# Attention beside a bilinear GLU on one core: moving the last split weights' store and the stores of the heads' outputs

## The chip, the core and the metric

The kernel runs on one core of a Trainium2 chip. The metric is device time in microseconds (us) of one execution. The kernel before took 2605.79 us, the median of 3 runs (2604.93 to 2606.27). A core has TensorE (PE, matmuls; PEld is its weight load), VectorE (DVE), ScalarE (ACT), GpSimd (POOL) and SyncE (SP). Each engine works through its own instructions in the order in which the program lists them, and waits on semaphores for the others. A DMA is issued by an instruction of SyncE or GpSimd: what stands behind an issue that waits, waits too.

## What is computed

```python
xn = layernorm(x)                        # x: 2048 x 576
q, k, v = split(xn @ wqkv)               # 32 heads of 18
s = concat_heads(softmax(q k^T / sqrt(18)) v) @ wo
h = (xn @ w_gate) * (xn @ w_up)          # 4608 columns
out = x + s * silu(h @ w_down)
```

All is float32. To keep its precision, matmul operands are split into a high part (float32r) and a low part (the rest), and a product is made of three partial products: high by high, high by low and low by high.

## The kernel before, in words

**Stages.** A first stage norms `x`, makes q, k and v and writes them to DRAM (`sqk`, `sv`). The long middle stage interleaves attention and the GLU in one stream of matmuls. The end multiplies the heads' outputs with `wo`, makes the gate's silu and writes the result.

**The GLU** goes over 72 units: 4 chunks of 512 rows of `x` (a pass each) times 18 blocks of 256 columns of F. A unit has two pairs of up and gate products (27 matmuls each, L658), and the down product of the unit before (L700), added to `acc` by DVE (L728). TensorE's upper and lower 64 rows work at the same time on two such streams (`stream(0)` for up, `stream(1)` for gate). The low part of `h` is made by GpSimd (L674); `turn_round` (L690) loads `hs` with its halves exchanged as `hx`.

In pass one (units 0 to 17) the weights are split as they are used: ScalarE makes the high part, GpSimd the low part (L191 for gate and up, L222 for down), and the split weights are stored in DRAM (`swg` at L196, `swd` at L226). The later passes load them (L182, L215). Odd passes take the blocks backwards, so that the unit after a pass turn (18, 36, 54) has the weights of the unit before and keeps its tile (L209 to L212). `d_get(u + 1)` is called in `down_end` when both halves of unit u's down product are listed, and `turn_round(u + 1, 1)` right after it (L735 to L738). At a pass turn the blocks of the next chunk of `x` are loaded, 18 DMAs (L358, L361).

**Attention.** Per head there are 64 "a" matmuls (L582), whose row maxima DVE takes (L584); `max_rows` sends them through GpSimd's queue (L604) into the stacked operands `pair` and `ring`; 64 "b" matmuls (L614), whose exponentials ScalarE takes (L616); and the product with v (L625), listed in visits of 7 blocks of 8 matmuls. `pair` and `ring` are loaded for each head by SyncE (L239). `finish(h)` transposes the head's sum on DVE, divides it by its last column, transposes it back into `oc` (L637 to L642), and stores it to `sot` with four DMAs of 18 rows by 512, one for each quarter of the rows (L645, SyncE).

**The order** is made when the program is written out, by `order()`. It keeps clocks for the two streams and for DVE, ScalarE and GpSimd, and one number, `queue[0]`, for when the DMA queue is through with what was issued. `moved(start, size)` adds a transfer to it at 0.24 MB per us and returns the time of landing, 2 us later. An operation is listed once its data are there by these clocks (`there`, `arrives`, `loaded`). In `visit`, when a head is finished, `queue[0]` is raised to the time at which DVE is through with the finish (L1034). Neither the stores of split weights nor the heads' stores are counted in `queue[0]`.

**The end.** When the last "b" is listed, `begin` puts six loads of the heads' outputs (`fetch_o`, L794) on a list `loads`; when the last visit is listed, `prefetch` adds four `fetch`es (L822, L824). `order()` lists one of them at a time, when `queue[0]` is at most 0.3 us ahead. What is left follows after the order, behind the loads of blocks 3 and 4 of the outputs (L794, L797). ScalarE makes the high part of each block (`high`, L802), DVE the low part (`low`, L807 and L809), `w_split` splits `wo` (L814, L815), and L1210 is the output projection: its first group of 6 products runs over four row tiles and two halves before the second begins.

Of the kernel before, what the change touches and what calls it, by code (L numbers as in the profile page):

```python
# [20 lines left out]
FT = mybir.dt.float32  # L21
# [19 lines left out]
def kernel(  # L41
# [10 lines left out]
    nc = tc.nc  # L52
    _, S, D = x.shape
    F = w_gate.shape[1]
    H = 32
    DH = D // H
# [3 lines left out]
    NF2 = F // 256  # L60
# [14 lines left out]
    swd = dram.tile([NF2, 128, 2, 2, 2, HALF], FT, name="swd")  # L75
    sv = dram.tile([S, H, DH + 1], FT, name="sv")
    sot = dram.tile([D, S], FT, name="sot")
# [49 lines left out]
    def d_tile():  # L127
        return wpool.tile([128, 2, 2, 2, HALF], FR, name="wd", bufs=1)
# [26 lines left out]
    def columns_of(u):  # L155
        c, q = units[u]
        return NF2 - 1 - q if c % 2 else q

    graw, gw, draw, dw = {}, {}, {}, {}
# [41 lines left out]
    def d_load(n):  # L201
        if n < NF2:
            draw[n] = d_raw(n)

    def d_get(n):
        if n >= len(units) - 1:
            return
        p = columns_of(n)
        if n and n % NF2 == 0:  # L209
            dw[n] = dw[n - 1]  # L210
            ddone.add(n)
            return  # L212
        w = dw[n] = d_tile()
        if n >= NF2:
            nc.sync.dma_start(w.bitcast(FT), swd[p])  # L215
            ddone.add(n)
            return
        raw = draw.pop(n)

        def dpiece(k):  # L220
            nc.scalar.activation(w[:, k, :, 0, :], raw[:, k], AF.Copy)
            nc.gpsimd.tensor_tensor(w[:, k, :, 1, :], raw[:, k], w[:, k, :, 0, :].bitcast(FT), op=OP.subtract)  # L222

        def end():
            ddone.add(n)
            nc.sync.dma_start(swd[p], w.bitcast(FT))  # L226
            d_load(n + 1)

        chores.extend([(dpiece, (k,)) for k in range(2)] + [(end, ())])
# [300 lines left out]
    for t in range(8, NT):  # L530
# [6 lines left out]
        if t > 11:  # L537
            for n in range(2 * (t - 12), 2 * (t - 11)):
                x_first(n // 2, n % 2)
    d_get(0)  # L540
    xg.append(xcp.tile([128, 9, 512], FR, name="xc"))
    n = 8
# [21 lines left out]
    with ExitStack() as mid:  # L564
# [55 lines left out]
        def pv_group(h, ts, k):  # L620

            p = bank("g", 1, k)
            for t in ts:
                for c in range(4):
                    nc.tensor.matmul(p[32 * c:32 * c + 32, :], vt[h // 2][:, t, 6 * (h % 2):6 * (h % 2) + 32], pt[t, c],  # L625
                                     start=t == ts[0], stop=t == ts[-1])
            if ts[0] == 0:
                oc[h] = mp.tile([128, 512], FT, name="oc", bufs=2)
                nc.scalar.activation(oc[h], p, AF.Copy)  # L629
            else:  # L630
                nc.vector.tensor_tensor(oc[h], oc[h], p, op=OP.add)  # L631

        def finish(h):
            o = oc.pop(h)
            d0 = 13 * (h % 2)
            tp = mp.tile([128, 512], FT, name="tp", bufs=1)
            nc.vector.transpose(tp, o)  # L637
            tr = tp.rearrange("p (j d) -> p j d", d=32)
            rc = mp.tile([128, NT, 1], FT, name="rc", tag="m", bufs=1)
            nc.vector.reciprocal(rc, tr[:, :, d0 + DH:d0 + DH + 1])  # L640
            nc.vector.tensor_tensor(tr[:, :, d0:d0 + DH], tr[:, :, d0:d0 + DH], rc.to_broadcast([128, NT, DH]), op=OP.mult)
            nc.vector.transpose(o, tp)  # L642

            for c in range(4):
                nc.sync.dma_start(sot[h * DH:(h + 1) * DH, 512 * c:512 * c + 512], o[32 * c + d0:32 * c + d0 + DH, :])  # L645

        hs, us = {}, {}
        TERMS = [t for b in range(9) for t in ((b, b, 0), (9 + b, b, 0), (b, b, 1))]
# [70 lines left out]
        def down_end(r, u, s, ps):  # L719
            c, q = units[u]  # L720
            cs = slice(r * HALF, (r + 1) * HALF)
            if q == 0 and c >= 2:
                ready(sdone, 4 * c - 8 + s)
            a = sums(4 * c + s)[:, cs]
            if q == 0:
                nc.vector.tensor_copy(a, ps[:, 0:HALF])
            else:
                nc.vector.tensor_tensor(a, a, ps[:, 0:HALF], op=OP.add)  # L728
            if q == NF2 - 1 and c < NCH - 1:
                seen[c, s] = seen.get((c, s), 0) + 1  # L730
                if seen[c, s] == 2:
                    silu_store(4 * c + s)
            if s == 3:
                seen[u] = seen.get(u, 0) + 1
                if seen[u] == 2:  # L735
                    d_get(u + 1)
                    if u + 1 < len(units) - 1:
                        turn_round(u + 1, 1)  # L738
# [50 lines left out]
        loads = []  # L789
# [90 lines left out]
        def next_free(tag):  # L880
            if tag == "g":
                return min(banks["g"])
            return banks[tag][turn[tag] % len(banks[tag])]

        def engine(eng, start, taken):
            free[eng] = max(free[eng], start) + taken
            return free[eng] + TAIL[eng]
# [14 lines left out]
        there, queue = {}, [0.0]  # L902
# [98 lines left out]
        def size(first):  # L1001
            h, t, _ = first
            n = h * NT + t
            whole = H * NT - LAST_BLOCKS
            return min(VISIT - n % VISIT, whole - n) if n < whole else 4 - (n - whole) % 4

        shown = [0.0]

        def visit(now):

            now = max(now, *clk)
            many = 0
            now += 0.095
            if due:
                now = max(now, next_free("g") - EARLY + 0.03)
            for h, t, at in due:
                if at > now + 0.5 * many + 0.3 or many == size(due[0]):
                    break
                now += 0.859
                many += 1  # L1020
            now -= 0.859 * many
            for h in sorted({h for h, _, _ in due[:many]}):
                ts = [t for g, t, _ in due[:many] if g == h]
                now = max(now, next_free("g") - EARLY + 0.03) + 0.859 * len(ts)
                k = banks["g"].index(next_free("g"))
                pv_group(h, ts, k)
                end = engine("DVE", now + 0.25, 0.60) if ts[0] else engine("ACT", max(now + 0.25, shown[0]), 0.495)
                banks["g"][k] = end + EARLY
                if ts[-1] == NT - 1:
                    finish(h)  # L1030
                    engine("DVE", end, 0.60)
                    engine("DVE", 0.0, 0.85)
                    shown[0] = engine("DVE", 0.0, 0.60)
                    queue[0] = max(queue[0], shown[0])  # L1034
            del due[:many]
            clk[0] = clk[1] = issued[0] = now + 0.13
            fresh[:] = True, True
# [40 lines left out]
        def order():  # L1078
# [5 lines left out]
            while any(heads) or na < TOTAL or nb < TOTAL or due:  # L1084
# [9 lines left out]
                if len(due) >= need and due[need - 1][2] <= now:  # L1094
                    wait = now if wait is None else wait
                    if abs(clk[0] - clk[1]) < 0.04 or now > wait + 1.0 or not all(heads):
                        visit(now if any(heads) else max([now] + [d[2] for d in due]))
                        wait = None
                        if nb == TOTAL and not due:
                            prefetch(now)  # L1100
                        continue
# [134 lines left out]
    for t in range(NT):  # L1236
# [5 lines left out]
        for _ in range((2, 0, 0, 0, 2, 2, 1, 0, 2, 2, 1, 0, 0, 0, 0, 0)[t]):  # L1242
            if split:
                k, c = split.pop(0)
# [35 lines left out]
```

## Time and profile before

| | before |
|---|---|
| median of 3 runs | 2605.79 us (2604.93 to 2606.27) |
| the profiled execution | 2606.23 us |
| its span, first to last instruction | 2604.5 us |
| granted TensorE clock, mean | 0.998 |
| busy: TensorE / DVE / ScalarE / GpSimd | 99% / 74% / 56% / 20% |
| read from and written to HBM | 312.21 MB, 107.61 MB |
| DMAs `sot<-oc`, L645 | 128, 36 KB each |
| DMAs `swd<-wd`, L226 | 18, 1152 KB each |

The profile is of one execution; its times count from the first instruction (us). A group of rows names line, engine and operation, then output <- input. "[3.86 <-DMA ring<-sqk]" behind an instruction says how long its engine stood idle before it and who released it. A trailing "q", as in SPq, is an engine's queue of semaphore and DMA-issuing instructions, which are not counted as busy. The granted clock is the share of full speed that TensorE was given.

### The profile page before, as it was taken

Reading aid. Unit: us, or ns where it says so; the run is one execution under the profiler, and the core shown is the slowest. Engines: PE = TensorE matmul, PEld = TensorE weight load, DVE = VectorE, ACT = ScalarE, POOL = GpSimd, SP = SyncE. Lnnn points to the kernel's source line nnn. Section 1 sums busy time; section 2 is a strip of 40 time slices with the busy share of each in tenths; the row PEclk is TensorE's granted clock in tenths of the full one; section 3 lists DMA queues with packets and bytes.
Section 4 is the critical chain, followed back from the end, with each engine's and each line's share of the span. In section 5 each row is a group of like instructions: output and inputs, shape, how many; then the busy total and the mean of one; then the engine's idle time right before and its main releaser. Section 6 shows DMA issues by size and latency. Waiting matters only on the chain.

```text
span 2604.5 us, 59060 instructions
## 1 busy us (share of the span) xinstructions
PE 2579.5 (99%) x24360; PEld 2115.4 (81%) x24360; DVE 1920.7 (74%) x3373; ACT 1462.6 (56%) x2698; POOL 526.3 (20%) x534
## 2 busy tenths in 40 slices
PE   8999999999999999999999999999999999999999
PEld 7899888788878888887888888877888888777879
DVE  6208777777767888877788788777788888777537
ACT  5222666666655555655555565655555665555551
POOL 3114433333311111101111111111010111111116
PEclk9999999999999999999999999999999999999999
DMA  7799989888785556565676556556685666655557
GB/s 234 224 287 269 268 225 225 229 217 222 218 204 164 175 178 178 172 179 165 177 191 178 165 173 182 176 164 174 158 204 154 176 184 175 177 175 167 152 165 251
DMA packets 194814, 504.57 MB, mean 194 GB/s; under 512 B 56360, under 2 KB 114344, under 8 KB 155504
## 3 DMA queue, kind: packets, MB, share of 16 engines
q1 hardware_dynamic: 188160, 492.15, 67.6%
q0 software_dynamic: 6384, 8.63, 1.2%
q8 instruction: 192, 3.15, 0.5%
q14 instruction: 78, 0.64, 0.1%
HBM read 312.21 MB, written 107.61 MB: 161 GB/s over the span
## 4 chain that ended last, share of the span: by engine, by line
PE 96%; DMA 2%; DVE 1%; issue 1%; ACT 1%; POOL 0%; SPq 0%; POOLq 0%; ACTq 0%; DVEq 0%
PE pg L658 34%; PE pg L625 17%; PE pg L700 15%; PE pa L582 11%; PE pb L614 9%; PE pg L392 2%; PE pa L338 2%; PE pb L338 2%; PE pg L1210 1%; PE pa L1210 1%; PE pb L1210 1%; DMA ring<-sqk 0%; DMA hx<-hs 0%; ACT xn L286 0%; DMA xc<-sx 0%
## 5 line engine op out<-in xcount | busy, mean ns | idle before, releaser
L584 DVE TENSOR_REDUCE mx<-pa 128x1 f32<-128x512 f32 x2048 | 1361.7, 684 | 161.5 <-PE pa L582 73.8
L616 ACT ACTIVATE pt<-pb 128x512 f32<-128x512 f32 x2048 | 1155.0, 597 | 567.8 <-PE pb L614 468.7
L658 PE MATMUL pg<-xc,wgu 64*128 64x512 f32 x7776 | 1396.6, 392 | 0.0
L658 PEld LDWEIGHTS pg<-xc,wgu 64*128 64x128 f32 x7776 | 1057.5, 186 | 45.5 <-issue 0.2
L614 PE MATMUL pb<-pair,ring 56*128 56x512 f32 x2006 | 788.9, 399 | 4.0 <-DMA ring<-sqk 3.9
L582 PE MATMUL pa<-pair,ring 54*128 54x512 f32 x2001 | 784.7, 398 | 0.3 <-DVE mx L584 0.3
L700 PE MATMUL pg<-wd,hs 64*128 64x288 f32 x3408 | 536.4, 292 | 1.2 <-DVE acc L728 1.2
L700 PE MATMUL pg<-wd,hx 64*128 64x288 f32 x3408 | 528.1, 292 | 1.3 <-DMA hx<-hs 1.2
L674 POOL TENSOR_TENSOR hs<-us,hs 128x512 fp32r<-128x512 f32 x144 | 186.3, 1294 | 1484.1 <-ACT hs L673 1442.9
L700 PEld LDWEIGHTS pg<-wd,hs 64*128 64x128 f32 x3408 | 473.5, 186 | 5.9 <-DVE acc L728 1.9
L700 PEld LDWEIGHTS pg<-wd,hx 64*128 64x128 f32 x3408 | 467.3, 185 | 5.2 <-DMA hx<-hs 2.0
L625 PE MATMUL pg<-pt,vt 128*32 128x512 f32 x4096 | 456.5, 596 | 0.0
L582 PEld LDWEIGHTS pa<-pair,ring 54*128 54x128 f32 x2001 | 363.4, 184 | 82.9 <-issue 48.6
L614 PEld LDWEIGHTS pb<-pair,ring 56*128 56x128 f32 x2006 | 364.7, 184 | 15.1 <-issue 5.1
L625 PEld LDWEIGHTS pg<-pt,vt 128*32 128x32 f32 x4096 | 125.9, 110 | 285.6 <-issue 282.0
L631 DVE TENSOR_TENSOR oc<-oc,pg 128x512 f32<-128x512 f32 x69 | 47.4, 687 | 325.2 <-PE pg L625 314.3
L728 DVE TENSOR_TENSOR acc<-acc,pg 128x288 f32<-128x288 f32 x544 | 233.8, 443 | 27.0 <-PE pg L700 24.2
L673 ACT ACTIVATE hs<-us 128x512 fp32r<-128x512 f32 x144 | 91.0, 632 | 154.5 <-DVE us L670 148.9
L191 POOL TENSOR_TENSOR wgu<-wraw,wgu 128x384 fp32r<-128x384 f32 x108 | 108.4, 1017 | 96.7 <-ACT wgu L190 66.3
L629 ACT ACTIVATE oc<-pg 128x512 f32<-128x512 f32 x32 | 19.2, 599 | 189.4 <-PE pg L625 183.6
L604 POOL DMA_DIRECT2D pair<-mt x128 | 76.6, 604 | 225.1 <-DVE mt L599 223.8
L670 DVE TENSOR_TENSOR us<-pg,us 128x512 f32<-128x512 f32 x144 | 98.2, 682 | 17.9 <-PE pg L658 14.4
(127 smaller groups left out, 1292.4 us busy)
## 6 DMA issues: line engine op xcount, KB each, us to landing
wgu<-swg SPq DMA_DIRECT2D x102, 1152.0 KB
hx<-hs SPq DMA_DIRECT2D x142, 512.0 KB
wd<-swd SPq DMA_DIRECT2D x50, 1152.0 KB
swg<-wgu SPq DMA_DIRECT2D x36, 1152.0 KB
pair<-sqk SPq DMA_DIRECT2D x192, 144.0 KB
ring<-sqk SPq DMA_DIRECT2D x384, 72.0 KB
swd<-wd SPq DMA_DIRECT2D x18, 1152.0 KB
sqk<-hl SPq DMA_DIRECT2D x32, 512.0 KB
```

The source lines that it names most:

```text
L191: nc.gpsimd.tensor_tensor(w[:, 9 + b:12 + b, :], raw[:, b:b + 3, :], w[:, b:b + 3, :].bitcast(FT), op=OP.subtract)
L338: nc.tensor.matmul(p, wq[b, a], xcs[c][:, e, :], start=n == 0, stop=n == len(PAIRS) - 1)
L582: nc.tensor.matmul(p, q[rows, t * 128:(t + 1) * 128], k[rows, c * 512:(c + 1) * 512], start=True, stop=True)
L584: nc.vector.tensor_reduce(mx[h][:, t, c:c + 1], p, axis=AX.X, op=OP.max)
L614: nc.tensor.matmul(p, k[rows, t * 128:(t + 1) * 128], q[rows, c * 512:(c + 1) * 512], start=True, stop=True)
L616: nc.scalar.activation(pt[t, c], p, AF.Exp, scale=scale)
L625: nc.tensor.matmul(p[32 * c:32 * c + 32, :], vt[h // 2][:, t, 6 * (h % 2):6 * (h % 2) + 32], pt[t, c], start=t == ts[0], stop=t == ts[-1])
L658: nc.tensor.matmul(ps, gw[n][half[r], a, :], xg[i][half[r], e, :], start=k == 0, stop=k == len(TERMS) - 1)
L670: nc.vector.tensor_tensor(h32, ps, h32, op=OP.mult)
L674: nc.gpsimd.tensor_tensor(hj[:, 1, :], h32, hj[:, 0, :].bitcast(FT), op=OP.subtract)
L700: nc.tensor.matmul(ps[:, 0:HALF], (hx if k else hs)[u][half[r], j, a, s * 128:(s + 1) * 128], dw[u][half[r], k, j, e, :], start=n == 0, st ...
L728: nc.vector.tensor_tensor(a, a, ps[:, 0:HALF], op=OP.add)
```

## The change

The store of the split down weights of block 17, the last of pass one, is no longer issued in unit 17's `end` but in `d_get(18)`, the first unit of pass two, which keeps the tile. The four stores of a head are issued by GpSimd for the first 31 heads; for the last head they are put on the list `loads` (0.037 MB each), to be issued by SyncE in their turn. The raise of `queue[0]` at the finish of a head is gone.

```diff
@@ d_get
         if n and n % NF2 == 0:
             dw[n] = dw[n - 1]
             ddone.add(n)
+            if n == NF2:
+                nc.sync.dma_start(swd[p], dw[n].bitcast(FT))
             return
...
         def end():
             ddone.add(n)
-            nc.sync.dma_start(swd[p], w.bitcast(FT))
+            if p < NF2 - 1:
+                nc.sync.dma_start(swd[p], w.bitcast(FT))
             d_load(n + 1)
@@ finish
+            def store(c, eng):
+                eng.dma_start(sot[h * DH:(h + 1) * DH, 512 * c:512 * c + 512], o[32 * c + d0:32 * c + d0 + DH, :])
+
             for c in range(4):
-                nc.sync.dma_start(sot[h * DH:(h + 1) * DH, 512 * c:512 * c + 512], o[32 * c + d0:32 * c + d0 + DH, :])
+                if h < H - 1:
+                    store(c, nc.gpsimd)
+                else:
+                    loads.append((store, (c, nc.sync), 0.037))
@@ visit
                     shown[0] = engine("DVE", 0.0, 0.60)
-                    queue[0] = max(queue[0], shown[0])
```

## The prediction

> **What bounds the kernel now.** I read the head of the page, then TensorE's waits over the whole span, then the two places that these waits name: the instructions of SyncE and TensorE in order of time, the chain, and short windows for the clock.
>
> ```profile
> span 2604.5 us, 59060 instructions
> PE 2579.5 (99%) x24360; PEld 2115.4 (81%) x24360; DVE 1920.7 (74%) x3373; ACT 1462.6 (56%) x2698; POOL 526.3 (20%) x534
> ```
>
> TensorE is busy for 99% of the span. A busy TensorE isn't one at its peak, but the order of its work is written out by a planner that always has another matmul to put beside a waiting one. So a DMA or another engine counts only where TensorE stood still for it. All waits of TensorE (engine, line, who was waited for: us in total, times, longest), those from the second row on:
>
> ```profile
> PE pb L614 <- DMA ring<-sqk: 3.9, 1, 3.9
> PE pa L1210 <- ACT hi L802: 2.1, 2, 1.4
> PE pg L700 <- DMA hx<-hs: 1.2, 1, 1.2
> ```
>
> One score matmul waited once for a load of `ring`, and the output projection waited for `hi` at its start. The third comes at about 281 us, before the first head is finished, where the change touches nothing. Everything rests on the first two.
>
> *The ring wait.* SyncE's DMA issues around it, in order of time (start, us, engine and line):
>
> ```profile
> 755.03 0.35 SPq L226 DMA_DIRECT2D swd<-wd  x1
> 755.43 1.87 SPq L239 DMA_DIRECT2D ring<-sqk  x3
> ```
>
> The three ring loads stand directly behind the store of the last split of down, L226. SyncE's own waits from 750 to 790 us say that this store also held the queue until GpSimd had made the split:
>
> ```profile
> SPq L226 <- POOL wd L222: 3.0, 1, 3.0
> ```
>
> The chain in order of time (start, us, what), an earlier undisturbed visit of PV first:
>
> ```profile
> 733.87 6.15 PE pg L625 x56
> ...
> 756.92 11.12 DMA ring<-sqk
> ...
> 768.79 7.97 PE pg L625 x56
> ```
>
> TensorE's instructions in order of time give the gap, and short windows (us, TensorE busy, granted clock, DMA share, GB/s) what came after it:
>
> ```profile
> 768.39 0.46 PE L614 MATMUL pb<-pair,ring 56*128 56x512 f32 x1 [3.86 <-DMA ring<-sqk]
> ```
>
> ```profile
> 768.00:772.00 4.00, 3.61 (x22) 0.68 0.40 131
> 772.00:776.00 4.00, 4.00 (x36) 0.89 0.02 4
> ```
>
> The wait costs twice: 3.86 us of standing still, and then the clock falls to 0.68, so that the 56 matmuls of the visit take 7.97 us where 6.15 us is normal, 1.82 us more. Together **5.68 us**.
>
> *The start of the output projection.* SyncE and ScalarE at the end of the planned order:
>
> ```profile
> 2522.61 0.45 SPq L794 DMA_DIRECT2D o<-sot  x1
> 2530.09 1.40 SPq L645 DMA_DIRECT2D sot<-oc  x4
> ```
>
> ```profile
> 2527.62 0.63 ACT L802 ACTIVATE hi<-o 128x512 fp32r<-128x512 f32 x1 [3.03 <-DMA o<-sot]
> ...
> 2535.38 0.63 ACT L802 ACTIVATE hi<-o 128x512 fp32r<-128x512 f32 x1 [6.55 <-DMA o<-sot]
> ```
>
> One of the six loads of the heads' outputs goes out at 2522.61; then SyncE stands until 2530.09 before the last head's stores, which wait for the transposes of `finish`. The other five loads queue behind them, and ScalarE waits 6.55 us for the second. What it costs is read off the first group of the projection, 4 row tiles x 2 halves x 6 = 48 matmuls (start of the first, start of the next group, an undisturbed dozen in the chain, and the clock):
>
> ```profile
> 2534.23 0.40 PE L1210 MATMUL pa<-wos,hi 128*128 128x288 f32 x1
> ...
> 2545.22 0.95 PE L1210 MATMUL pa<-wos,o 128*128 128x288 f32 x6
> ```
>
> ```profile
> 2546.96 1.59 PE pg L1210 x12
> ```
>
> ```profile
> 2538.00:2542.00 4.00, 3.86 (x19) 0.63 0.99 315
> ```
>
> A dozen takes 1.59 us, so 48 need 6.36; they took 10.99. **4.63 us** are lost, part waits and part the clock of 0.63.
>
> **A page against the rows.** The Trainium skill, page "TensorE: Matmul & The Clock Gate", section "What's actually happening", lets the clock fall to half after an idle window of about 3.4 us. The ring wait agrees with that; at the projection the longest single wait was 1.4 us and the clock fell all the same. Taken strictly, the rule would leave the end only its waits of some 2.3 us (an estimate) and the sum near 8.0 instead of 10.3; the row with 0.63 decides.
>
> **The change part by part.**
>
> *Last split's store in pass two.* It removes from L226 one DMA and with it the 3.0 us of SyncE's wait. Its size, and the rate of the stretch before the gap (windows; the last two figures are DMA share and GB/s):
>
> ```profile
> swd<-wd SPq DMA_DIRECT2D x18, 1152.0 KB
> ```
>
> ```profile
> 755.00:768.40 13.40, 9.54 (x84) 9.03 (x80) 8.89 (x14) 7.39 (x13) 1.29 (x2) 1.00 0.98 260
> ```
>
> The DMA engines are full (0.98), so what counts is bytes ahead, not the earlier issue: 1152 KB are 1.18 MB, at 260 GB/s 4.5 us. The load landed at 768.04 and would land at 763.5; TensorE wants it at 768.39 - 3.86 = 764.5. The wait goes, with 1 us to spare, and nothing else was late: the following visit had its data. From both sides: nothing, if the later loads crowd in; 5.68 at most. I take 5.68, since the bytes stand ahead in the same queue. If a rest of a microsecond stays, it costs only itself: the 1.2 us wait for `hx` left the clock alone.
>
> ```profile
> 278.00:282.00 4.00, 2.75 (x32) 1.00 0.98 308
> ```
>
> The store comes back in `d_get(18)`, called by `down_end` of unit 17 just ahead of the next `hx` issue:
>
> ```profile
> 790.50 1.11 SPq L690 DMA_DIRECT2D hx<-hs  x2
> ```
>
> ```profile
> 810.57 0.29 PE L700 MATMUL pg<-wd,hs 64*128 64x288 f32 x1
> ```
>
> It puts 4.5 us ahead of that `hx`, whose first reader starts at 810.57, 20 us after the issue. In every other unit of the later passes a load of the same size stands there. It costs nothing; without that cover it would cost 4.5 us.
>
> *Stores of 31 heads through GpSimd.* SyncE loses 124 issues and its longest class of waits that isn't for a buffer:
>
> ```profile
> SPq L645 <- DVE oc L642: 197.0, 29, 13.4
> ```
>
> That is 6.8 us a head by which loads behind can go earlier. Since TensorE waited for a load only twice in the whole planned stage, this gains nothing now. GpSimd takes on 124 DMA issues. Its nearest row (shortest, median and longest ns of one, first and last start in us):
>
> ```profile
> L604 POOL DMA_DIRECT2D pair<-mt x128: 594/597/769, 250.6 to 2445.3; - x128
> ```
>
> 124 x 0.597 = 74 us on an engine that is busy for 526 of 2604; 2.4 us a head. GpSimd now stands before the stores until DVE's transposes are through, and behind them in its queue wait `hs` low parts, in pass one the splits (L191, L222), `silu`'s products, and `pair<-mt`. What stood behind one head's stores (SyncE's row, then GpSimd's):
>
> ```profile
> 779.78 1.36 SPq L645 DMA_DIRECT2D sot<-oc  x4
> ```
>
> ```profile
> 782.63 1.29 POOL L674 TENSOR_TENSOR hs<-us,hs 128x512 fp32r<-128x512 f32 x1 [20.57 <-ACT hs L673]
> ```
>
> Four issues from 779.78 on would end at 782.2, in front of it. Its result goes out with the `hx` at 790.50, 6.6 us after it is done, and is read at 810.57. I cost the move at zero; bounds below.
>
> The Trainium skill, page "SBUF — State Buffer", section "SBUF: two separate sides", speaks against the move: while DVE holds the port that it shares with GpSimd, the latter can't write descriptors, and a DMA of 620 ns took 3100. At that price a head's stores would hold GpSimd for 12.4 us (an estimate from the page). The longest of the 128 issues here, 769 ns, shows nothing of the sort, so the chances don't move.
>
> *The last head behind the loads.* The stores join the list of loads after the six of `begin`, so five loads go out before SyncE stands, 7.0 + 1.4 = 8.4 us earlier. The first, issued at 2522.61, was there for ScalarE at 2527.62; at 260 GB/s each 0.262 MB takes 1.0 us, so all six are there by about 2532.7, before 2534.23. The stores themselves go no later: they wait for DVE. So the 4.63 us go. What is late next is DVE, which has no gap between these two rows:
>
> ```profile
> 2549.76 0.69 DVE L807 TENSOR_TENSOR o<-o,hi 128x512 fp32r<-128x512 f32 x1 [5.28 <-ACT hi L802]
> ...
> 2594.74 0.46 DVE L1219 TENSOR_TENSOR ys<-pg,gl 128x288 f32<-128x288 f32 x1 [0.88 <-PE pg L1210]
> 2596.65 0.46 DVE L1219 TENSOR_TENSOR ys<-pg,gl 128x288 f32<-128x288 f32 x1 [1.46 <-PE pg L1210]
> ```
>
> If the load that starts this stretch came no earlier, only DVE's last gaps, 0.88 + 1.46 = 2.34 us, could be won. But five loads (1.31 MB) have left the queue ahead of it, at the 315 GB/s of that time 4.2 us. I take 4.63 with 2.34 as the low end.
>
> *The planner's line.* Without the raise of `queue[0]` the plan lets loads land up to DVE's finish earlier, which is now so. All order after the first head can come out another, of the same work. No row shows the new order. TensorE has almost no other wait to win (I allow 1 us), and a loss would be a new wait like the ring's, 5.7 us at the upper end. I take zero.
>
> **The sum**: 5.68 + 4.63 = 10.3 us. The profiled execution took 2606.23 us, its span and 1.73 around it; that is 0.44 above the median of the runs, 2605.79. 2606.23 - 10.3 = **2595.9 us**.
>
> **The rivals.**
>
> 1. *One wait stays or a new one comes.* The pass turn carries 4.7 MB of `x` blocks with full DMA engines and the margin is 1 us; or the new order lets some other score matmul run into a late load. Either way the gain is the end's alone: 2606.23 - 4.63 = 2601.6. For it speaks the margin, against it that the other two pass turns, which have no such store, made TensorE wait for no load.
> 2. *DVE holds the end.* 5.68 + 2.34: 2598.2.
> 3. *The order at the end and at the turn comes out such that the loads don't move*; the change then only shifts issues: 2605 to 2606.
> 4. *Slower: GpSimd's queue passes the wait on.* In pass one SyncE already waits for GpSimd's splits:
>
> ```profile
> SPq L196 <- POOL wgu L191: 90.2, 23, 10.1
> ```
>
> If splits stand behind waiting stores, SyncE stands before L196 with ring loads behind it. Price: 6.8 + 2.4 = 9.2 us for each of the six heads whose L645 rows stand ahead of the turn, 55 us at most. It decides once more than 10.3 + 5.2 = 15.5 us of it reach TensorE, 2.6 a head. With half of it: 2606.2 - 10.3 + 27.6 = 2623.5. Against it: those 90.2 us cost TensorE nothing now, and before, SyncE itself stood there for the same transposes.
>
> **How the numbers follow.** Forecast 0.58; DVE at the end 0.10; one wait stays or comes 0.17; no effect 0.07; slower 0.08. The range: 2593, for the forecast with the odd wait won and some scatter, to 2602, for the first rival; about 0.8 lie in it. 0.2% is 5.2 us, about what a measurement here can tell from no change, so faster means below 2600.6. Forecast, the DVE case and 0.05 of the first rival: 0.73 faster; 0.19 the same; 0.08 slower.
>
> **What would show it.** TensorE's waits without `ring<-sqk` at the turn, and without L802 at the projection; the visit after the turn at 6.15 us with a clock of 1.00; the 48 matmuls in about 6.4 us; no L226 store beside the eighteenth `x` block; five loads of `o` ahead of the last head's stores; GpSimd busy by some 74 us more, its waits now for L642. It would be wrong with a new TensorE wait for a DMA or for `hs`, or a DVE without gaps to the very end.

## The result, and the profile after

| | before | after |
|---|---|---|
| median | 2605.25 us (20 runs, 2602.54 to 2608.30) | 2600.68 us (20 runs, 2598.43 to 2603.92) |
| ratio, 95% interval | 1 | 0.9982 [0.9975, 0.9989] |
| the profiled execution / its span | 2606.23 / 2604.5 us | 2602.83 / 2601.1 us |
| DMAs issued by GpSimd | 159 | 283 |

The change makes the kernel 4.6 us faster by the medians, 0.18%. That is a gain, since the interval leaves 1 out, but it is less than half of the forecast's 10.3 us and just inside the 0.2% that I had called no change. Lines below are those of after: the code around the change stands 3 to 9 lines lower (PV L628, "b" L617, down L709, the projection L1218, the heads' stores L648). Lines of an experiment are those of its own kernel.

The head of after's page. GpSimd's queue (q0: packets, MB, share of the DMA engines) is a line that the prediction does not use; before, it had 6384 packets.

```profile
span 2601.1 us, 59086 instructions
PE 2576.5 (99%) x24360; PEld 2109.3 (81%) x24360; DVE 1919.9 (74%) x3373; ACT 1462.6 (56%) x2698; POOL 590.7 (23%) x658
...
q0 software_dynamic: 10352, 13.22, 1.9%
```

GpSimd is busy for 64 us more; the busy times of the other engines moved by 0.3% at most. TensorE's waits over the whole span (engine, line, who was waited for: us in total, times, longest):

```profile
PE pg L320 <- ACT xn L289: 6.9, 1, 6.9
PE pb L617 <- DMA ring<-sqk: 2.2, 1, 2.2
...
PE pg L709 <- DVE acc L737: 1.2, 2, 0.7
...
PE pg L709 <- DMA hx<-hs: 0.4, 1, 0.4
...
PE pg L667 <- DMA xc<-sx: 0.3, 1, 0.3
```

The wait for `hi` at the projection is gone. The wait for `ring` at the pass turn is not: 2.2 us are left of 3.9, although the store that stood ahead of it now goes out elsewhere. The chain around it (start, us, what), and the clock behind it (window, us, TensorE busy, granted clock, DMA share, GB/s):

```profile
752.74 12.96 DMA ring<-sqk
...
765.84 0.40 PE pb L617
766.24 7.97 PE pg L628 x56
```

```profile
764.00:768.00 4.00, 2.16 (x18) 0.90 0.66 226
768.00:772.00 4.00, 4.00 (x32) 0.67 0.07 19
```

The visit still takes 7.97 us, at a clock of 0.67. So in this execution the turn kept most of its loss. The other place did what it was meant to do. SyncE's issues at the end of the planned order, then the chain in the projection:

```profile
2519.94 3.83 SPq L803 DMA_DIRECT2D o<-sot  x6
2527.41 1.75 SPq L648 DMA_DIRECT2D sot<-oc  x4
```

```profile
2531.58 1.79 PE pa L1218 x12
2533.37 1.59 PE pb L1218 x12
2534.97 3.19 PE pg L1218 x24
2538.15 0.79 PE pa L1218 x6
```

All six loads of `o` go out ahead of the stores. The first group's 48 matmuls run from 2531.58 to 2538.15, 6.57 us where they took 10.99.

**Where the time went.** I cut both traces at the same four points: the start of the last PV visit ahead of the pass turn (733.80 before, 732.43 after; the visit after it is the one behind the ring load), the start of the second visit behind it, the start of the last visit of all, and the end of DVE's last instruction.

| stretch | before | after | difference |
|---|---|---|---|
| up to the last visit ahead of the turn | 733.80 | 732.43 | -1.37 |
| the turn | 69.12 | 67.62 | -1.50 |
| middle, to the start of the last visit | 1720.40 | 1720.59 | +0.19 |
| the end, to DVE's last instruction | 76.22 | 72.13 | -4.09 |
| DVE's last instruction to the end of the span | 4.92 | 8.28 | +3.36 |

They add to -3.4, the difference of the spans, 2604.5 and 2601.1. The first row holds the stores of six heads, so the change does touch it; but this point lies between 732.0 and 733.8 us in all fourteen kernels measured here, on the mean 0.2 us apart between those with these stores on GpSimd and those with them on SyncE, so I read it as scatter. The last row is the surprise. DVE, the last engine to compute, is done 6.77 us earlier, but the program ends only 3.4 us earlier. The closing line of the program, before and then after (line, engine, operation, times: shortest, median and longest ns, first and last start):

```profile
L1275 POOLq DRAIN  x3: 40/102/4750, 2598.6 to 2604.2; - x3
```

```profile
L1283 POOLq DRAIN  x3: 40/102/8418, 2591.9 to 2600.8; - x3
```

When GpSimd has nothing left to do, it drains before it meets the other engines at the end. That took 4.75 us and now takes 8.42. SyncE's row for the end shows the others standing there; its releaser (PE) is misnamed, TensorE was long done:

```profile
SPq L1283 <- PEq L1283: 5.8, 2, 5.3
```

### The profile page after: what moved, and what is told of

It is laid out like the page before. It is cut to its first block, busy times and chain, and to the rows that moved or that the text cites. A ratio compares the mean times of both kernels' runs of the same rounds, so it can differ in the third digit from the quotient of the medians.

```text
span 2601.1 us, 59086 instructions
## 1 busy us (share of the span) xinstructions
PE 2576.5 (99%) x24360; PEld 2109.3 (81%) x24360; DVE 1919.9 (74%) x3373; ACT 1462.6 (56%) x2698; POOL 590.7 (23%) x658
## 4 chain that ended last, share of the span: by engine, by line
PE 97%; DVE 1%; DMA 1%; ACT 0%; SPq 0%; issue 0%; ACTq 0%; DVEq 0%
PE pg L667 34%; PE pg L628 17%; PE pg L709 16%; PE pa L585 11%; PE pb L617 9%; PE pg L395 2%; PE pa L341 2%; PE pb L341 2%; PE pg L1218 1%; PE pa L1218 1%; PE pb L1218 1%; DMA ring<-sqk 0%; DMA hx<-hs 0%; ACT xn L289 0%; DMA xin<-in_A_x_dram 0%
## 5 line engine op out<-in xcount | busy, mean ns | idle before, releaser
L617 PE MATMUL pb<-pair,ring 56*128 56x512 f32 x2006 | 789.1, 399 | 2.2 <-DMA ring<-sqk 2.2
L709 PE MATMUL pg<-wd,hs 64*128 64x288 f32 x3408 | 536.6, 292 | 1.2 <-DVE acc L737 1.2
L709 PE MATMUL pg<-wd,hx 64*128 64x288 f32 x3408 | 528.6, 292 | 0.4 <-DMA hx<-hs 0.4
L709 PEld LDWEIGHTS pg<-wd,hs 64*128 64x128 f32 x3408 | 473.4, 186 | 5.8 <-DVE acc L737 1.9
L709 PEld LDWEIGHTS pg<-wd,hx 64*128 64x128 f32 x3408 | 467.8, 185 | 4.4 <-DMA hx<-hs 1.0
L628 PE MATMUL pg<-pt,vt 128*32 128x512 f32 x4096 | 456.5, 596 | 0.0
L617 PEld LDWEIGHTS pb<-pair,ring 56*128 56x128 f32 x2006 | 364.7, 184 | 14.4 <-issue 3.4
L628 PEld LDWEIGHTS pg<-pt,vt 128*32 128x32 f32 x4096 | 125.9, 110 | 285.8 <-issue 281.9
L648 POOL DMA_DIRECT2D sot<-oc x124 | 64.1, 523 | 332.8 <-DVE oc L645 330.7
```

The lines of the kernel that those rows point to most:

```text
L617: nc.tensor.matmul(p, k[rows, t * 128:(t + 1) * 128], q[rows, c * 512:(c + 1) * 512], start=True, stop=True)
L709: nc.tensor.matmul(ps[:, 0:HALF], (hx if k else hs)[u][half[r], j, a, s * 128:(s + 1) * 128], dw[u][half[r], k, j, e, :], start=n == 0, st ...
```

## The experiments

My theory after the result: the gains at the two places add, and each is read from its own stretch; the turn's gain came out small because fewer bytes ahead of the ring load shortened its way less than I had reckoned; and 3.4 to 3.7 us are given back by GpSimd's closing drain, which the 124 stores moved to its queue make longer. The rivals: the ring load is late because the plan lists it too early or with `hx` ahead of it; and the new order, not the drain, took the rest. Each ratio is from 5 to 20 executions of the kernel. "A" is the store of the split weights moved, "B" the 31 heads' stores through GpSimd, "C" the last head's stores behind the loads.

| kernel | start of visit to start of next, turn | that next visit | end | closing drain | ratio to before, 95% |
|---|---|---|---|---|---|
| before | 34.98 | 7.91 | 76.2 | 4.75 | 1 |
| after (A, B, C) | 33.80 | 7.91 | 72.1 | 8.42 | 0.9982 [0.9975, 0.9989] |
| u1_store (B, C) | 36.02 | 8.65 | 72.3 | 8.42 | 0.9993 [0.9984, 1.0002] |
| u2_last (A, B) | 33.20 | 6.22 | 76.0 | 8.42 | 1.0003 [0.9994, 1.0012] |
| s5_sync (A, C) | 33.27 | 6.22 | 71.9 | 4.95 | 0.9980 [0.9971, 0.9989] |
| a8_alone (A) | 32.75 | 6.21 | 77.1 | 4.58 | 0.9989 [0.9980, 0.9998] |
| g10_alone (B) | 35.14 | 8.59 | 76.6 | 8.42 | 1.0010 [1.0002, 1.0019] |
| c9_alone (C) | 35.46 | 7.90 | 71.7 | 4.76 | 0.9989 [0.9980, 0.9998] |
| d6_double (A, B in two halves, C) | 34.86 | 6.22 | 72.1 | 4.58 | 0.9977 [0.9967, 0.9987] |
| h12_half (A, half of B, C) | 34.69 | 6.22 | 72.6 | 5.40 | 0.9976 [0.9967, 0.9985] |
| p3_plan (A, B, C, plan) | 31.10 | 6.21 | 78.7 | 8.33 | 1.0003 [0.9994, 1.0012] |
| h4_hx (A, B, C, `hx` behind) | 32.87 | 6.22 | 71.5 | 8.42 | 0.9980 [0.9972, 0.9989] |
| b7_best (A, C, `hx` behind) | 31.50 | 6.21 | 71.5 | 4.72 | 0.9967 [0.9955, 0.9979] |
| b11_outs (b7, outputs by SyncE) | 33.42 | 6.22 | 71.5 | 6.80 | 0.9963 [0.9951, 0.9976] |

Columns two to five are us from one profiled execution each, so a single row scatters by a microsecond; I read the groups. The stretch between the second visit behind the turn and the last visit is 1720.0 to 1720.7 in all fourteen.

### Undo the moved store (u1_store)

```diff
-            if n == NF2:
-                nc.sync.dma_start(swd[p], dw[n].bitcast(FT))
             return
...
-            if p < NF2 - 1:
-                nc.sync.dma_start(swd[p], w.bitcast(FT))
+            nc.sync.dma_start(swd[p], w.bitcast(FT))
```

> The changed kernel with the first part undone: the store of the last split of down goes out in unit 17 again, ahead of the ring loads at the first pass turn, and none in unit 18. In the trace of the changed kernel TensorE still waits 2.17 us for that ring load (3.86 before), and the visit behind it still takes 7.9 us. Theory P (the plan prices the turn's transfers too low, and the store's own share of the lateness is small): the wait goes from 2.2 to some 3 to 4 us, the visit stays at 7.9, the time rises by 1 to 2 us over the changed kernel's. Rival Q (the store was worth its 4.5 us, and another part of the change, GpSimd's stores or SyncE's freed queue, gave some 3 us of it back): the ring load lands 4.5 us later than in the changed kernel, the wait is 6 to 7 us and the time rises by 4 to 5 us.

TensorE's wait for `ring` is 3.5 us again:

```profile
PE pb L614 <- DMA ring<-sqk: 3.5, 1, 3.5
```

The visit behind it is slow too, 8.65 us. The time is 2604.05 us beside 2606.15 of before; against after's ratio that is +2.9 us, with 3.0 either way. The wait is the one that theory P names, not the 6 to 7 us of rival Q. The time alone neither proves that the move is worth something nor rules out 5.68; a8_alone, below, does both.

### Undo the last head's place (u2_last)

```diff
-                    loads.append((store, (c, nc.sync), 0.037))
+                    store(c, nc.sync)
```

> The changed kernel with the last part undone: the last head's four stores are issued by SyncE where finish lists them, ahead of the remaining loads for the end. If the end's gain is its own (the traces show the first 48 matmuls of the projection in 6.6 us after, 11.0 before): 4 to 4.5 us slower than the changed kernel, with TensorE waiting for L802-like highs again. If a store at that place no longer matters because the loads go out earlier anyway without the raise of the queue's clock: within 1 us.

The wait for `hi` is back, and so is the order in SyncE's queue:

```profile
PE pa L1218 <- ACT hi L811: 1.6, 2, 0.9
```

```profile
2518.66 0.45 SPq L803 DMA_DIRECT2D o<-sot  x1
2526.15 1.37 SPq L648 DMA_DIRECT2D sot<-oc  x4
2527.76 2.29 SPq L803 DMA_DIRECT2D o<-sot  x5
```

The end takes 76.0 us instead of 72.1, and the whole gain is gone: 2606.42 us beside 2606.15. Against after that is +5.5 us, 3.0 either way. What is left, A and B, can't be told from nothing.

### A truer size in the plan (p3_plan)

```diff
-                                there["x", c + 1, k // 3, r] = moved(clk[r] + 0.5, 0.262)
+                                there["x", c + 1, k // 3, r] = moved(clk[r] + 0.5, 0.32)
```

The plan counts an `x` block at 0.262 MB and 0.24 MB per us; counted larger, the ring load is due later and the plan lists other matmuls first.

> The changed kernel with the plan's size of an x block raised from 0.262 to 0.32 MB, so that the plan expects the ring load at the turn some 4.3 us later; DMAs and their order stay. Theory P (the plan is wrong by some 4 us there): TensorE's order puts other matmuls ahead, its wait for ring goes, the visit takes 6.2 us, and the kernel is 3 to 4.5 us faster than the changed one, near 2597. Rival R (there is no other work to list at the turn, all streams depend on x or ring): the plan leaves the gap itself, the time stays within 1 us.

The wait for `ring` is gone and the turn is the shortest of all. But later decisions came out otherwise, too, and DVE is waited for in new places:

```profile
PE pg L709 <- DVE acc L737: 3.2, 4, 1.3
PE pa L585 <- DVE mx L587: 2.0, 3, 1.2
```

The last visit now starts 3.95 us earlier than in after, but the end takes 78.7 us instead of 72.1. Counted in the traces, TensorE does 87 down matmuls behind the start of the last visit, where after and before do none. The time is 2606.08 us: the 4 us of the turn, and more, are lost at the end. So the wait depends on the plan's number, but changing that number gains nothing.

### The hx of unit 17 behind the ring loads (h4_hx)

```diff
-                    if u + 1 < len(units) - 1:
+                    if u + 2 == NF2:
+                        chores.append((turn_round, (u + 1, 1)))
+                    elif u + 1 < len(units) - 1:
                         turn_round(u + 1, 1)
```

> The changed kernel with the hx loads of unit 17 (1.05 MB, from SBUF to SBUF) listed behind the ring loads of the turn instead of ahead of them; TensorE's order is the same. If the ring loads wait for the bytes of hx in SyncE's queue: they land 4 to 6 us earlier, the 2.17 us wait and the slow visit go, 3 to 4.5 us faster than the changed kernel, near 2597. If the load is late because of the x blocks alone: it lands at most 1 us earlier and the wait stays above 1 us, time within 1.5 us.

After's two `hx` DMAs, 512 KB each, stood directly ahead of the ring loads in SyncE's queue; here they stand behind:

```profile
749.83 1.50 SPq L242 DMA_DIRECT2D ring<-sqk  x3
752.36 1.73 SPq L699 DMA_DIRECT2D hx<-hs  x2
```

No wait for `ring` is left, and the waits for `hx` (0.5 us) and for `x` blocks (1.3) stay small. The time, 2600.76 us beside 2606.15, can't be told from after's ratio; the 3 to 4.5 us expected did not come. The profile shows where some of it stayed: DVE's last instruction ends 3.5 us earlier than in after (2589.28 against 2592.77), but GpSimd's last DMA goes out only 0.7 us earlier (2591.17 against 2591.88), and 8.42 us of drain are counted from there.

### The heads' stores back to SyncE (s5_sync)

```diff
-                    store(c, nc.gpsimd)
+                    store(c, nc.sync)
```

> The changed kernel with the stores of the first 31 heads issued by SyncE again; the other parts stay, and TensorE's order is that of the changed kernel. The traces so far show GpSimd's closing drain, an instruction behind its last DMA, at 4.75 us in the kernel before (155 DMAs through its queue) and at 8.42 us in every kernel with 279. Theory D (the drain costs some 30 ns for each DMA that went through GpSimd's queue): the drain is back at 4.75 us and the kernel is 3.7 us faster than the changed one, near 2597, with the gain at the end kept. Rival E (the drain's length comes from the end itself, say from what is in flight): it stays above 7 us and the time within 1 us. Rival F (SyncE's waits for the finishes come back and cost TensorE): new waits of TensorE for DMAs, not faster.

(The expectations speak of 155, 279 and 403 DMAs of GpSimd; with four of `ring<-mt` the traces have 159, 283 and 407.) The drain is short again:

```profile
L1283 POOLq DRAIN  x3: 40/102/4950, 2591.1 to 2596.6; - x3
```

The profiled span is 2596.9 us, 4.2 less than after's, 3.5 of it the drain. The median is 2599.79 us beside 2605.25; against after's ratio -0.5 us, 3.0 either way, far less than the 3.7 us expected; it neither proves the 3.4 us of the drain nor quite leaves them out. This run also had a ring wait like after's, and no loss of clock behind it:

```profile
766.71 0.46 PE L617 MATMUL pb<-pair,ring 56*128 56x512 f32 x1 [2.25 <-DMA ring<-sqk]
```

```profile
768.00:772.00 4.00, 4.00 (x44) 1.00 0.18 39
```

### GpSimd's stores alone (g10_alone)

This is the kernel before with one edit:

```diff
-                nc.sync.dma_start(sot[...], o[...])
+                (nc.gpsimd if h < H - 1 else nc.sync).dma_start(sot[...], o[...])
```

> The kernel before with the stores of the first 31 heads through GpSimd and nothing else; TensorE's order is that of the kernel before. Theory D: drain 8.4 us and 3.7 us slower than before, near 2609.5; the two waits of TensorE as before. Rival (SyncE's freed queue gains something along the way): within 1.5 us of before or faster.

Both old waits are as they were (3.5 us for `ring`, 2.0 for `hi`), and the drain is after's to the nanosecond:

```profile
PE pb L614 <- DMA ring<-sqk: 3.5, 1, 3.5
PE pa L1210 <- ACT hi L802: 2.0, 2, 1.3
```

```profile
L1275 POOLq DRAIN  x3: 40/102/8418, 2599.0 to 2607.9; - x3
```

2608.42 us beside 2605.25; by the ratio that is slower by 2.6 us, interval 0.5 to 5.0. The third part of the change, by itself, costs time.

### Each GpSimd store in two (d6_double)

(8418 - 4750) / 124 is 30 ns for each added DMA. If that is what a drain costs, 124 more DMAs make it 12 us.

```diff
-                    store(c, nc.gpsimd)
+                    for i in (0, 9):
+                        nc.gpsimd.dma_start(sot[h * DH + i:h * DH + i + 9, ...], o[32 * c + d0 + i:32 * c + d0 + i + 9, :])
```

> The changed kernel with each of the 124 stores through GpSimd cut in two of 9 rows: 248 more issues than the kernel before, the same bytes and the same rows. Theory D: the drain grows by another 124 x 30 ns to 12.1 us and the kernel is 3.7 us slower than the changed one, near 2604.5. If the drain goes by rows or bytes instead of by DMAs: it stays at 8.4 us, time within 1 us.

```profile
L1285 POOLq DRAIN  x3: 40/102/4577, 2591.5 to 2596.5; - x3
```

With 407 DMAs the drain is the shortest of all. My price by the DMA has fallen. The time, 2598.92 us beside 2605.25, can't be told from after's ratio.

### hx behind and the stores on SyncE (b7_best)

The edits of h4_hx and s5_sync together.

> The changed kernel with the heads' stores back on SyncE and the hx loads of unit 17 behind the ring loads: what the experiments point to. Drain 4.75 us, no ring wait at the turn and a visit of 6.2 us behind it, the projection's first 48 matmuls in 6.6 us: some 4 us faster than the changed kernel by the drain and 1 to 2 by the turn, 2594 to 2597, so below both kernels.

No wait for `ring`, the visit at full clock, the short drain:

```profile
764.00:768.00 4.00, 4.00 (x40) 1.00 0.73 259
768.00:772.00 4.00, 4.00 (x40) 1.00 0.05 10
```

```profile
L1285 POOLq DRAIN  x3: 40/102/4716, 2588.1 to 2593.4; - x3
```

2596.13 us beside 2605.25, 0.9967: faster than both kernels of this case, and near the time that I had forecast for the change.

### The moved store alone (a8_alone), the last head alone (c9_alone)

Both start from the kernel before. a8_alone takes over the `d_get` and `end` hunks of the change; c9_alone this:

```diff
+                if h < H - 1:
+                    store(c)
+                else:
+                    loads.append((store, (c,), 0.037))
...
-                    queue[0] = max(queue[0], shown[0])
+                    if h < H - 1:
+                        queue[0] = max(queue[0], shown[0])
```

> The kernel before with the moved store of the last split of down and nothing else. So far the traces of kernels with the moved store have the ring load land some 1.2 us earlier, counted from the visit before the turn, than those with the store in unit 17, and the turn as a whole, up to the second visit behind it, 3.4 us shorter on the mean (1.5 to 3.8). If the parts add up: 2 to 4 us faster than before, with a ring wait of 0 to 2.3 us left and the drain at 4.75 us. If the first prediction's size were right (5.7 us): 5 to 6 us faster and no wait.

> The kernel before with the last head's stores put behind the loads for the end (and the raise of the queue's clock left out for that head alone), nothing else. If the end's gain is its own: from the last visit to the last DVE instruction 72.1 us instead of 76.2, 4 us faster than before, drain 4.75 us, the ring wait as before.

Each shows its own wait gone, or nearly (0.6 us for `ring` are left in a8_alone), and the other's still there, a8_alone first:

```profile
PE pa L1213 <- ACT hi L805: 2.1, 2, 1.4
...
PE pb L617 <- DMA ring<-sqk: 0.6, 1, 0.6
```

```profile
PE pb L614 <- DMA ring<-sqk: 4.1, 1, 4.1
```

The medians, 2602.14 and 2602.13 us beside 2605.20, are 0.9989 each: 2.9 us apiece, 0.5 to 5.2. With B's +2.6 the three parts add to -3.2; the change measured -4.7 by its ratio, within the scatter of three such intervals. These two also complete a set: before, a8_alone, g10_alone, c9_alone, u2_last, s5_sync, u1_store and after have every combination of A, B and C. Averaged over the four pairs that differ in one part (the planner's line aside), A measures -2.5 us, B +2.0 and C -3.8, each some 1.6 either way (an estimate from the intervals of the single ratios). They add to -4.3. So the parts add, A is worth less than 5.68, and B costs time, by these times rather less than the drain's 3.7.

### Half of the heads through GpSimd (h12_half)

```diff
-                    store(c, nc.gpsimd)
+                    store(c, nc.gpsimd if h < 16 else nc.sync)
```

> The changed kernel with GpSimd's queue for the first 16 heads only, SyncE's for the rest: 64 more DMAs through GpSimd instead of 124. The drain was 4.75, 8.42 and 4.58 us at 155, 279 and 403 DMAs, so it doesn't grow by the DMA. If it goes by where the queue's ring stands at the end: anything between 4.5 and 8.4, and not by the proportion. If it has two values only, one for an idle queue and one for something left to fetch or to write back: 4.6 to 5.0 or 8.3 to 8.5. By the proportion it would be 6.6.

```profile
L1283 POOLq DRAIN  x3: 40/102/5400, 2592.0 to 2597.9; - x3
```

223 DMAs give 5.40 us, where a straight line between 159 and 283 would give 6.6. The time is 2598.22 us beside 2605.20.

### The last outputs by SyncE (b11_outs)

b7_best, and the outputs of the last tiles leave GpSimd's queue, so that its last DMA is issued long before it drains:

```diff
-            nc.gpsimd.dma_start(out2[t * 128:(t + 1) * 128, :], y)
+            (nc.sync if t >= NT - 4 else nc.gpsimd).dma_start(out2[t * 128:(t + 1) * 128, :], y)
```

> The fastest kernel so far (heads' stores on SyncE, hx of unit 17 behind the ring loads) with the outputs of the row tiles 12 to 14 issued by SyncE instead of GpSimd, so that GpSimd's last DMA is that of tile 11, some 8 us before its last other instruction. If the drain waits for DMAs in flight: it falls below 2 us and the end comes 2 to 3 us earlier, near 2593.5. If it is a fixed cost: 4.7 us, the same time as the fastest.

```profile
L1285 POOLq DRAIN  x3: 40/238/6797, 2585.7 to 2593.6; - x3
```

GpSimd's instructions ahead of it (the last DMA, and the last adds):

```profile
2579.32 0.58 POOL L1236 DMA_DIRECT2D out_dram<-ys  x1 [0.30 <-POOL ys L1234]
...
2585.36 3.38 POOL L1234 TENSOR_TENSOR ys<-ys,xi 128x288 f32<-128x288 f32 x4
```

The row of 6.80 us begins at 2585.7 and runs beside the adds until 2588.74; 3.8 us lie behind them. In before the same part, behind the last issue, is 4.2 us, as the row of 4.75 begins with that issue, of 0.56. Since the last DMA here was issued 5.8 us before the drain began, the drain is not a wait for the data of that DMA. 2595.62 us, 0.9963: the fastest kernel here, not to be told from b7_best.

## Why the prediction was half right, point by point

**Right: the two places, the end, and what was costed at nothing else.** The end takes 71.9 us on the mean of the nine kernels with C (p3_plan's other order left out) and 76.5 on the mean of the four without: 4.5 us, beside the 4.63 of the sum. DVE did not hold it. Its last gaps, 0.88 and 1.46 us before, are there still, so the stretch ahead of them came earlier:

```profile
2587.51 0.46 DVE L1227 TENSOR_TENSOR ys<-pg,gl 128x288 f32<-128x288 f32 x1 [0.39 <-PE pg L1218]
2589.43 0.46 DVE L1227 TENSOR_TENSOR ys<-pg,gl 128x288 f32<-128x288 f32 x1 [1.46 <-PE pg L1218]
```

The planner's line, taken at zero, was zero: the middle differs by 0.19 us. Counted in the traces, TensorE begins every visit with the same numbers of GLU, attention and PV matmuls behind it in all kernels but p3_plan, with the planner's line or without; so a new order took nothing either. The store in pass two stood ahead of the next `hx` and TensorE waited for nothing there:

```profile
781.00 0.34 SPq L213 DMA_DIRECT2D swd<-wd  x1
787.64 1.12 SPq L699 DMA_DIRECT2D hx<-hs  x2
```

The slower rival, GpSimd's queue passing waits on, did not come. GpSimd's issues took 64.1 us, 523 ns each where I had taken 597, and it stood for DVE's transposes 330.7 us in total. SyncE's wait for its splits rose from 90.2 to 113.9 us. None of it reached TensorE:

```profile
L648 POOL DMA_DIRECT2D sot<-oc x124 | 64.1, 523 | 332.8 <-DVE oc L645 330.7 <-issue 2.1
```

```profile
SPq L196 <- POOL wgu L191: 113.9, 25, 12.2
```

**Failed: "1152 KB are 1.18 MB, at 260 GB/s 4.5 us ... The wait goes, with 1 us to spare, and nothing else was late."** The term of 5.68 us was mis-sized. On the mean of the four kernels with the store in unit 17 and the six with only the store moved (h4_hx, b7_best, b11_outs and p3_plan left out), the visit behind the turn starts 35.40 and 33.76 us after the one ahead of it, 1.64 less where I had 3.86. The visit itself takes 8.26 and 6.50 us, 1.76 less where I had 1.82. TensorE's wait for `ring` is 3.5 to 4.1 us in the four and 0 to 2.3 us in the six. So the clock's part was right, the wait's was not, and together it is 3.4 us (3.8 on the mean of the four pairs that differ in A alone, the planner's line aside); after's own profile, with 1.50, is the one of the six in which the clock fell all the same.

The rate is a part of why. Short windows of the kernel before, when the store was under way, and then of after at the same place (the last two figures are DMA share and GB/s):

```profile
761.00:763.00 2.00, 1.00 0.94 367
763.00:765.00 2.00, 1.00 1.07 372
```

```profile
761.00:763.00 2.00, 1.00 1.10 173
763.00:765.00 2.00, 1.00 0.87 199
```

The DMA engines are about full in both. The mean of 260 GB/s mixed stretches of different rates: the one with the store ran at 370, and 1.18 MB at 370 GB/s are 3.2 us, not 4.5. The packets in the traces give nearly that. In before 128 packets of 9216 bytes start between 759.9 and 763.8, most of them 347 ns long; they are taken for the store's, which was issued 4 us ahead of the next transfer with packets of this size. Shared by the 16 DMA engines they are 3.0 us of work, and 2.9 to 3.0 in the other three kernels that have the store there. In after the ring loads' packets run in these windows, and beside them those of the next weights, issued behind them and of 9216 bytes too:

```profile
758.35 0.35 SPq L182 DMA_DIRECT2D wgu<-swg  x1
```

These took 450 to 1070 ns each for the most part until the ring loads' packets were through (764.6), and about 350 ns from 765.3 on. So the rate went with what ran side by side, not with the kind of transfer. Even the 3.0 us did not arrive in full: the ring load landed 34.5 us after the start of the last visit ahead of the turn on the mean of the four with the store (768.04 - 733.80 = 34.24 in before), and 33.1 us on the mean of five with it moved (765.70 - 732.43 = 33.27 in after), 1.5 us earlier. Why not more is not settled. And it was not true that nothing else was late: TensorE now waited for `x` blocks, up to 1.9 us (h12_half). The other 1.05 MB ahead, `hx`, matter by the traces: with them behind, no ring wait is left in h4_hx, b7_best and b11_outs, where one of the six has none, and the turn is 1.4 us shorter again on the mean of the three (64.9 against 66.3 us). The times do not tell this apart from nothing: b7_best against s5_sync is -3.4 us, 3.9 either way.

**Failed: "I cost the move at zero"**, for the 124 stores. The prediction started from "a DMA or another engine counts only where TensorE stood still for it". That leaves out what comes behind TensorE's last matmul. It followed GpSimd's queue through the middle, where zero holds, and not to the end of the program, though the drain stood in the trace of before with 4750 ns. All six kernels with 283 DMAs of GpSimd show 8.33 to 8.42 us; the five with 159 show 4.58 to 4.95. B alone measures +2.6 us [0.5, 5.0].

With the terms as measured, -3.4 (turn) - 4.5 (end) + 3.7 (drain) = -4.2 us, beside the 4.7 of the ratio and the 10.3 of the sum. Rival 1, "one wait stays", had named 2601.6 us, and the time is 2600.68; but that rival was only half of the reason. That the time lies in the range is in part luck: its upper end, 2602, stood for one wait that stays whole, and what came was a wait that stayed in part and a drain that no rival had named.

**Open:** what sets the length of the drain. It is not the number of DMAs (4.58 us at 407), not their bytes (d6_double moved 13.2 MB through q0 like after), and not what GpSimd's queue still has in flight: its last packet is through at 2594.25 in after, 6.0 us before the drain ends, at 2601.01 in before, 2.4 us before, and in b11_outs at 2581.37, before the drain begins. Why after itself and s5_sync, with ring waits of 2.17 and 2.25 us, differ in the clock behind it isn't settled either.

## What to carry to other kernels

When work moves to another engine's queue, follow that engine to the last line of the program: its closing drain is on everybody's path, and no wait of TensorE shows it. When a transfer is taken from ahead of a late load, cost its bytes at the rate of the short windows in which it runs, not at the mean of a longer stretch, and ask which other bytes stand ahead or run beside; here, with two `hx` DMAs listed behind the load as well, no wait for it was left. A fix in the order by hand at the one place (h4_hx, 0.9980) was worth more than another constant in the plan (p3_plan, 1.0003), because the constant moved later decisions too.

## What the runs showed of the hardware that I had not expected

- GpSimd's closing drain takes 4.6 to 8.4 us and depends on what its queue carried in the whole program, in no simple way. The Trainium skill, page "VectorE: DVE Perf Modes", section "The DRAIN you can't avoid", knows of drains at the start and end of a program as about 12 ns on all engines. SyncE's here agree, at 7 ns; GpSimd's differ, as do the longest of TensorE (2.6 us) and ScalarE (3.2 us) in after, and the measurement decides. That page counts some 57 such drains in a kernel, where the closing line has two or three for each engine here, so it may mean others.
- A wait of 2.17 us was enough once to bring the clock down to 0.67, and one of 2.25 us left it at 1.00. The waits of 3.5 to 4.1 us cost clock in all four kernels that had them. The Trainium skill, page "TensorE: Matmul & The Clock Gate", section "What's actually happening", has the clock fall after an idle window of about 3.4 us and lets that window run on freely, not from the start of a wait. The second part would let equal waits end differently, as they do here; a fall after 2.17 us of standing still is less than it asks for.
- At a DMA share of about 1.0, the rate was 370 GB/s in one stretch and 173 in another, so a full share does not tell the rate. Packets of 9216 bytes took 347 ns where little ran beside them and up to 1070 ns beside the ring loads.
